# Moving VectorE's part of the weights' decoding within a unit of work, in a top-k attention and cosine feed-forward kernel on one Trainium2 core

## The chip, the cores and the metric

The kernel runs on one core of one Trainium2 chip. A core has five engines that run side by side, each through its own list of instructions in order: TensorE (PE, with its weight loads shown apart as PEld), VectorE (DVE), ScalarE (ACT), GpSimd (POOL) and SyncE (SP), which here only issues transfers. They wait for each other through semaphores. The metric is the device time of one execution in microseconds (us); lower is better. The figure for the kernel before is the median of several runs, 1549.34 us. The profile is of one further execution.

## The reference

There are two stages. For every one of 8 x 8 pairs of batch and head, attention over 576 positions keeps the 32 highest scores of each row. Its output, laid out as 4608 rows (tokens) of 512, goes through a feed-forward layer with 2048 hidden columns whose gate is `h * cos(h)`.

```python
scores = (1 / sqrt(D)) * matmul(q, k.transpose(0, 1, 3, 2))      # D = 64, S = 576
kth = partition(scores, -32)[..., -32]
scores = where(scores >= kth, scores, -1e9)
scores = scores - max(scores)
attn = exp(scores)
attn = attn / (sum(attn) + 1e-9)
x = matmul(attn, v)              # brought to (4608, 512)
h = x @ w_in                     # (512, 2048)
out = (h * cos(h)) @ w_out       # (2048, 512)
```

`q`, `k` and `v` arrive as float32. The two weight matrices arrive as 64-bit floats; the kernel turns them into float32 itself. This is "the decoding".

## The kernel before

**Units and slots.** A unit is 128 rows (tokens) of two heads: 36 blocks of 128 tokens by 4 pairs of heads give 144 units. The loop runs once for each unit and once more; a turn of it is called a slot. What the engines do in a slot, and in which order, is written out by hand: the order of the calls in `early_slot`, `slot` and `last_slot` is the order of each engine's instructions. Slots 0 to 12 are `early_slot` (`EARLY = 3 * NP = 12`), slots 13 to 140 `slot`, the last four `last_slot`. In slot i the unit u = i has its top-k search made; w is unit i - 1, which had its search in the slot before and is now finished.

**The search (VectorE).** `topk_first(u, w)` folds the 576 scores of each row in two halves of 288 (L244, one maximum and one minimum, read from PSUM and from ScalarE's copy in SBUF), closes the threshold of the unit before (`merge_first` L292, `merge_second` L297), and makes the first round of the search: `MAX8` (L304) gives the eight largest, `MATCH_REPLACE8` (L307) strikes them out. `topk_round(u, 1)`, `(u, 2)` and `(u, 3)` are the other rounds.

**Finishing the unit before.** `bounds`, `mask` and `exponentials` are ScalarE's (L314, L317, L326, L334); they end with `den` at L339. VectorE's `reciprocal` (L343) turns `den` into `rden`. GpSimd's `normalise` (L348) waits for it; then in early slots TensorE transposes the result (`transposes_now`, L382), ScalarE copies it out of PSUM (L386, L389), TensorE multiplies it with the values (L408), and ScalarE copies that out (`take_values`, L414). In ScalarE's list that copy stands ahead of `bounds` of the next slot. So from one reciprocal to the next there runs a loop through GpSimd, TensorE and ScalarE.

**The decoding.** There are 32 chunks of 128 x 512 (16 of `w_in`, 16 of `w_out`), and each goes through four stations. `load_weights(n)` issues up to n transfers on SP's queue into staging tiles (L116). `decode_first(n)` is three ScalarE activations for a chunk (L126 to L128). `decode_second(n)` is two VectorE `tensor_scalar` instructions for a chunk: a maximum with 2.0 (L137), in place on the float32 chunk, and a shift left by 3 (L138), in place on the same bits. `decode_third()` is two GpSimd `tensor_tensor` for every chunk that has had its second part (L147, L148). It stands in GpSimd's list behind `normalise` and `gate`. Of the chunks, slot 0 decodes three, slots 1 to 5 three each, slots 6 to 12 two each: 3 + 15 + 14 = 32. After slot 12 nothing is left to decode.

**GpSimd's list in an early slot** is therefore: `normalise` (L348, twice), `gate` (L530) where there is one, `decode_third`, then `reduce_first` (L504, L505, L506) and `reduce_second` (L513) where a tile of hidden columns is ready. After that it waits for the next slot's reciprocal.

**The feed-forward part** is spread over the slots by `feed`, which takes as many steps as a credit allows. All these choices are made while the program is built, so the order of the instructions does not depend on how long anything takes.

Of the kernel before, what the change touches and what calls it, by code (L numbers as in the profile page):

```python
# [31 lines left out]
def kernel(  # L32
# [70 lines left out]
    def load_weights(n):  # L103
        for _ in range(n):
            i = wq["next"]
            if i >= len(chunks):
                return
            src, dst = chunks[i]
            if not DECODE:
                nc.sync.dma_start(out=dst, in_=src)  # L110
                wq["next"] = wq["done"] = i + 1
                continue
            if staged() + ff["live"] >= CHUNKS:
                return
            st = ffw.tile([P, CW, 2], I32, tag="g", name="st", bufs=CHUNKS)
            nc.sync.dma_start(out=st.rearrange("p w i -> p (w i)"), in_=src)  # L116
            wq["loaded"].append((st, dst))
            wq["next"] = i + 1
# [12 lines left out]
    def decode_second(n):  # L131


        for _ in range(min(n, len(wq["second"]))):
            st, w = wq["second"].popleft()
            wi = w.bitcast(I32)
            nc.vector.tensor_scalar(out=w, in0=w, scalar1=2.0, scalar2=None, op0=ALU.max)  # L137
            nc.vector.tensor_scalar(  # L138
                out=wi, in0=wi, scalar1=3, scalar2=None, op0=ALU.logical_shift_left
            )  # L140
            wq["third"].append((st, w))

    def decode_third():
        while wq["third"]:
            st, w = wq["third"].popleft()
            wi = w.bitcast(I32)
            nc.gpsimd.tensor_tensor(out=wi, in0=wi, in1=st[:, :, 0], op=ALU.add)  # L147
            nc.gpsimd.tensor_tensor(out=w, in0=w, in1=st[:, :, 1].bitcast(F32), op=ALU.mult)  # L148
            wq["done"] += 1
# [63 lines left out]
    def scores(u):  # L213
        sc = u["sc"] = ps.tile([P, 2, 512], F32, tag="sc", name="sc", bufs=2)
        for to, k0, k1 in ((sc, 0, SB), (sc_ends[u["n"] % 2], SB, S)):
            for j in range(2):
                d = slice(j * D, (j + 1) * D)
                for b, q0, rows, r0 in u["parts"]:
                    st = pairs[b, u["hp"]]
                    nc.tensor.matmul(  # L220
                        to[r0 : r0 + rows, j, 0 : k1 - k0],
                        st["q"][d, q0 : q0 + rows],
                        st["k"][d, k0:k1],
                        start=True,
                        stop=True,
                    )

    def take_scores(u):
        s = u["s"] = work.tile([P, 2, S], F32, tag="s", name="s", bufs=4)
        nc.scalar.copy(out=s[:, :, 0:SB], in_=u["sc"][:, :, 0:SB])  # L230
        nc.scalar.copy(out=s[:, :, SB:S], in_=sc_ends[u["n"] % 2])  # L231
        if not u["folds"]:
            del u["sc"]
# [23 lines left out]
    def topk_first(u, w):  # L257

        u["top"] = tops[u["n"] % len(tops)]
        merges = [merge_first, merge_second] if w and w["folds"] else []  # L260
        if u["folds"]:
            for op in (ALU.max, ALU.min):
                fold(u, op)
                if merges:
                    merges.pop(0)(w)
        else:
            u["rest"] = work.tile([P, 2, S], F32, tag="rest", name="rest", bufs=1)
        for merge in merges:
            merge(w)
        topk_round(u, 0)  # L270

    def topk_round(u, rnd):
        top, rest, lasts = u["top"], u["rest"], TOPK // 8 - 1
        end = TOPK - 1 - 8 * rnd
        at = top[:, :, end : end - 8 if rnd < lasts else None : -1, 0]
        if u["folds"]:
            search(at, rest[:, :, 0:HS], rest[:, :, 0:HS], rnd < lasts)
            if rnd < TOPK // 16:

                low = top[:, :, 1 + 8 * rnd : 9 + 8 * rnd, 1]  # L280
                search(low, rest[:, :, HS:S], rest[:, :, HS:S], rnd < TOPK // 16 - 1)
        else:
            search(at, u["s"] if rnd == 0 else rest, rest, rnd < lasts)
        if rnd == lasts:
            del u["rest"]
# [23 lines left out]
    def bounds(u):  # L309

        ends = u.pop("top").rearrange("p j r i -> p j (r i)")
        ends = ends[:, :, 2 * TOPK - 2 :] if u["folds"] else ends[:, :, 2 * TOPK - 2 :: 2 - 2 * TOPK]
        nb = u["nb"] = small.tile([P, 2, 2], F32, tag="nb", name="nb")
        nc.scalar.mul(out=nb, in_=ends, mul=-SCALE)  # L314
        nd = u["nd"] = small.tile([P, 2], F32, tag="nd", name="nd")
        for j in range(2):
            nc.scalar.activation(  # L317
                out=nd[:, j : j + 1], in_=ends[:, j, 1:2], func=AF.Identity,
                bias=nb[:, j, 0:1], scale=SCALE,
            )  # L320

    def mask(u):

        s, nb = u["s"], u.pop("nb")
        for j in range(2):
            nc.scalar.activation(  # L326
                out=s[:, j], in_=s[:, j], func=AF.Prelu, bias=nb[:, j, 1:2], scale=SCALE, alpha=FAR
            )

    def exponentials(u):  # L330
        s, nd = u["s"], u.pop("nd")
        den = u["den"] = small.tile([P, 2], F32, tag="den", name="den")
        for j in range(2):
            nc.scalar.activation(  # L334
                out=s[:, j], in_=s[:, j], func=AF.Exp, bias=nd[:, j : j + 1], scale=1.0,
                accum_out=den[:, j : j + 1],
            )

        nc.scalar.activation(out=den, in_=den, func=AF.Identity, bias=eps, scale=1.0)  # L339

    def reciprocal(u):
        u["rden"] = small.tile([P, 2], F32, tag="rden", name="rden")
        nc.vector.reciprocal(u["rden"], u.pop("den"))  # L343

    def normalise(u):
        s, rden = u["s"], u.pop("rden")
        for j in range(2):
            nc.gpsimd.tensor_scalar(  # L348
                out=s[:, j], in0=s[:, j], scalar1=rden[:, j : j + 1], scalar2=1.0,
                op0=ALU.mult, op1=ALU.mult,  # L350
            )
# [130 lines left out]
    def take_banks():  # L482
        while full:
            take, *what = full.popleft()
            take(*what)
# [22 lines left out]
    def reduce_second():  # L508
        if not fresh or len(fresh[0]) < 3:
            return  # L510
        blk, g, x = fresh.popleft()
        if not ff["end"]:
            nc.gpsimd.tensor_tensor(out=x, in0=g, in1=x, op=ALU.subtract)  # L513
        waiting.append((blk, g, x, ff["now"], -TWO_PI_BELOW if ff["end"] else TWO_PI_BELOW))
# [11 lines left out]
    def gate(n):  # L526
        for _ in range(min(n, len(sined))):
            blk, g, x = sined.popleft()
            eng = nc.vector if ff["end"] else nc.gpsimd
            eng.tensor_tensor(out=g, in0=g, in1=x, op=ALU.mult)  # L530
            blk["gated"].append(ff["tick"])
# [81 lines left out]
    for n in range(NP, len(order)):  # L613
        i = last[order[n - 5]] if n >= 5 else 0
        at_slot.setdefault(max(i, NP + 2), []).append((load_qk, *order[n]))
        i = last_values[order[n - 6]] if n >= 6 else 0
# [12 lines left out]
    def early_slot(i, u, w):  # L629
        n = 3 if i < 6 else 2  # L630
        topk_first(u, w)
        decode_second(1 if i == 0 else n)
        scores(units[i + 1])
        for load, b, hp in at_slot.get(i, []):
            load(b, hp)
        load_weights(n)
        if w:
            bounds(w)
            mask(w)
            exponentials(w)  # L640
        topk_round(u, 1)
        if i == 0:
            decode_second(2)
        if w:
            reciprocal(w)
        topk_round(u, 2)
        topk_round(u, 3)
        if w:
            normalise(w)
        take_banks()  # L650
        take_scores(units[i + 1])
        gate(1)
        decode_third()
        feed(2)
        reduce_first()
        reduce_second()
        if i != NP:
            decode_first(n - 1)
        if w:
            transposes_now(w)  # L660
        feed(1)
        decode_first(n - len(wq["second"]))
        if w:
            values([w])
            take_values([w])
        feed(2)
        sines(1)
# [167 lines left out]
```

## Time and profile before

| | |
|---|---|
| time, median of 7 runs | 1549.34 us (1546.88 to 1551.63) |
| time of the profiled execution | 1556.08 us |
| its span, first to last instruction | 1554.3 us |
| TensorE's mean granted clock in it | 0.947 of full speed |
| ACT busy | 1171.3 us, 75% of the span |
| POOL busy | 1097.1 us, 71% of the span |
| L137, 32 instructions | 411 ns at least, 1368 ns at most |
| L138, 32 instructions | 426 ns at least, 2458 ns at most |

The profiled execution lies 6.7 us above the median of the runs, and 1.8 us of it lie outside its span. An engine's busy time counts an instruction from its start to its end, so time in which an instruction stands blocked inside the engine counts as busy. A timeline gives for each instruction its start and its duration in us, then engine, line and operation, then what it writes and reads; what stands in brackets is the engine's idle time ahead of it and what ended that. Spans on POOL are rough.

In the profiled execution the early slots begin (first fold of VectorE) at 7.63, 20.72, 32.67, 46.41, 60.17, 73.92, 88.20, 102.15, 117.57, 132.98, 150.83, 163.58 and 179.00 us; slot 13 begins at 193.47 us.

### The profile page before, as it was taken

The page shows a single profiled execution, that of the slowest core. Times are in us where ns is not written, and L with a number is a line of the kernel's source. Part 1 is how long each engine was busy: PE and PEld are TensorE (multiplying, and loading weights), DVE is VectorE, ACT ScalarE, POOL GpSimd, SP SyncE. Part 2 cuts the span into 40 slices and gives each one's busy share as a digit, 9 for nine tenths or more (in the row PEclk, how much of TensorE's full clock was granted, in tenths as well). Part 3 has the DMA queues.
Part 4 walks back from the last instruction along what each step waited for, and adds up shares of the span by engine and source line. Part 5 has one row for each costly group of instructions (what it writes and reads, how often), then busy time and mean ns, then how long its engine had stood idle before and what let it go on. Part 6 is the DMA issues. An engine that isn't in the chain of part 4 may idle for free.

```text
span 1554.3 us, 30369 instructions
## 1 busy us (share of the span) xinstructions
PE 1438.4 (93%) x10396; PEld 1031.2 (66%) x10396; DVE 1428.1 (92%) x4809; ACT 1171.3 (75%) x2342; POOL 1097.1 (71%) x834
## 2 busy tenths in 40 slices
PE   4477798999999999999999999999999999999999
PEld 3364565667667776777677776777677776777675
DVE  7998986999999998999999998999999999999831
ACT  7788775788778886788788886888788887888651
POOL 4666675777777777777777776777777777777510
PEclk6587988999999999999999999999999999999999
DMA  8331136545654456545655455545654455544300
GB/s 255 111 109 41 42 72 171 137 137 150 184 161 130 130 146 169 147 132 153 181 143 134 139 148 160 153 137 145 180 147 137 129 147 173 145 130 130 83 8 14
DMA packets 361835, 207.51 MB, mean 134 GB/s; under 512 B 311888, under 2 KB 328528, under 8 KB 361680
## 3 DMA queue, kind: packets, MB, share of 16 engines
q1 hardware_dynamic: 356272, 195.91, 45.5%
q10 hardware_dynamic: 5408, 9.65, 1.7%
q8 instruction: 82, 1.34, 0.4%
q14 instruction: 73, 0.60, 0.1%
HBM read 45.09 MB, written 84.93 MB: 84 GB/s over the span
## 4 chain that ended last, share of the span: by engine, by line
POOL 31%; DVE 26%; PE 21%; issue 10%; ACT 6%; DMA 5%; SPq 1%; POOLq 0%; ACTq 0%; DVEq 0%
DVE top L304 10%; POOL halves L360 8%; DVE rest L307 8%; PE mm L465 7%; PE o L543 7%; POOL s L348 6%; POOL g L530 5%; POOL x L513 4%; DVE rest L244 4%; PE rim L408 3%; PE sc L220 3%; DMA pT<-rows 2%; POOL x L506 2%; POOL x L505 2%; DMA rows<-halves 2%
## 5 line engine op out<-in xcount | busy, mean ns | idle before, releaser
L304 DVE MAX8 top<-rest 128x8 f32<-128x288 f32 x1716 | 692.7, 457 | 0.0
L465 PEld LDWEIGHTS mm<-xT,w_in 128*128 128x128 f32 x4608 | 542.8, 194 | 69.8 <-issue 62.4
L543 PE MATMUL o<-w_out,g 128*128 128x512 f32 x1152 | 546.3, 608 | 7.4 <-POOL g L530 3.9
L465 PE MATMUL mm<-xT,w_in 128*128 128x128 f32 x4608 | 546.4, 277 | 2.6 <-ACT g L478 2.5
L307 DVE MATCH_REPLACE8 rest<-top,rest 128x288 f32<-128x288 f32 x1144 | 504.3, 452 | 0.0
L348 POOL TENSOR_SCALAR s<-s,rden 128x576 f32<-128x576 f32 x288 | 212.4, 749 | 330.5 <-DVE rden L343 323.0
L543 PEld LDWEIGHTS o<-w_out,g 128*128 128x128 f32 x1152 | 204.8, 192 | 199.9 <-issue 183.4
L360 POOL COPY halves<-s 128x2304 uint16<-128x2304 uint16 x128 | 269.3, 2104 | 9.5 <-DMA rows<-halves 1.5
L244 DVE TENSOR_TENSOR rest<-sc,s 128x576 f32<-128x576 f32 x284 | 213.8, 753 | 39.1 <-ACT s L231 31.1
L334 ACT ACTIVATE s<-s,nd 128x576 f32<-128x576 f32 x288 | 220.5, 767 | 1.2 <-ACT ob L553 0.4
L326 ACT ACTIVATE s<-s,nb 128x576 f32<-128x576 f32 x288 | 206.0, 763 | 0.0
L408 PE MATMUL rim<-pT,v 128*64 128x128 f32 (+1 forms) x2560 | 166.8, 276 | 29.2 <-DMA pT<-rows 19.4
L408 PEld LDWEIGHTS rim<-pT,v 128*64 128x64 f32 x2560 | 137.0, 143 | 84.5 <-issue 39.6
L220 PE MATMUL sc<-k,q 64*128 64x448 f32 (+1 forms) x640 | 160.1, 605 | 13.2 <-DVE w_in L138 7.1
L530 POOL TENSOR_TENSOR g<-g,x 128x1024 f32<-128x1024 f32 x68 | 160.8, 2364 | 7.4 <-ACT nb L314 4.0
L513 POOL TENSOR_TENSOR x<-g,x 128x1024 f32<-128x1024 f32 x68 | 160.8, 2364 | 5.7
L478 ACT ACTIVATE g<-mm 128x512 f32<-128x512 f32 x144 | 84.6, 588 | 93.9 <-PE mm L465 88.0
L230 ACT COPY s<-sc 128x896 f32<-128x896 f32 x144 | 129.6, 900 | 4.9 <-PE sc L220 4.9
L414 ACT COPY xT<-rim 128x256 f32<-128x256 f32 (+1 forms) x80 | 28.0, 350 | 111.6 <-PE rim L220 92.7
L523 ACT ACTIVATE x<-x,halfpi 128x1024 f32<-128x1024 f32 x72 | 83.0, 1152 | 25.2 <-POOL x L513 17.9
L220 PEld LDWEIGHTS rim<-k,q 64*128 64x128 f32 (+1 forms) x640 | 59.7, 187 | 61.3 <-issue 56.4
L307 DVE MATCH_VALUE_LOAD rest<-top,rest 128x8 f32 x1144 | 96.6, 84 | 0.0
(55 smaller groups left out, 1261.5 us busy)
## 6 DMA issues: line engine op xcount, KB each, us to landing
rows<-halves SPq DMA_DIRECT2D x128, 576.0 KB, 2.8
out_dram<-ob ACTq DMA_DIRECT2D x36, 256.0 KB, 2.7
q<-in_q_dram SPq DMA_DIRECT2D x31, 288.0 KB, 3.4
st<-in_moe_w_in_dram SPq DMA_DIRECT2D x16, 512.0 KB, 5.2
v<-in_v_dram SPq DMA_DIRECT2D x32, 256.0 KB, 3.2
st<-in_moe_w_out_dram SPq DMA_DIRECT2D x16, 512.0 KB, 3.6
k<-in_k_dram SPq DMA_DIRECT2D x31, 144.0 KB, 3.5
k<-in_k_dram SPq DMA_DIRECT2D x32, 128.0 KB, 3.4
```

What stands on the lines that cost most here:

```text
L220: nc.tensor.matmul(to[r0 : r0 + rows, j, 0 : k1 - k0], st["q"][d, q0 : q0 + rows], st["k"][d, k0:k1], start=True, stop=True,)
L244: nc.vector.tensor_tensor(out=u["rest"][:, :, i * HS : (i + 1) * HS], in0=sc[:, :, 0:HS], in1=s[:, :, HS:S], op=op,)
L304: nc.vector.max(to[:, j], src[:, j])
L307: nc.vector.match_replace(rest[:, j], to[:, j], src[:, j], NEG)
L334: nc.scalar.activation(out=s[:, j], in_=s[:, j], func=AF.Exp, bias=nd[:, j : j + 1], scale=1.0, accum_out=den[:, j : j + 1],)
L348: nc.gpsimd.tensor_scalar(out=s[:, j], in0=s[:, j], scalar1=rden[:, j : j + 1], scalar2=1.0, op0=ALU.mult, op1=ALU.mult,)
L360: nc.gpsimd.tensor_copy(out=halves, in_=s.rearrange("p (k h) -> p h k", h=2))
L408: nc.tensor.matmul(o[d, to], lhsT, rhs, start=c == 0, stop=c == NT)
L465: nc.tensor.matmul(mm[:, at : at + w], w_in[f // FC][:, c, (f % FC) * P : (f % FC + 1) * P], blk["xT"][:, c], start=c == 0, stop=c == NC - 1,)
L513: nc.gpsimd.tensor_tensor(out=x, in0=g, in1=x, op=ALU.subtract)
L530: eng.tensor_tensor(out=g, in0=g, in1=x, op=ALU.mult)
L543: nc.tensor.matmul(o, g[:, at : at + P], w_out[f], start=f == 0, stop=f == NF - 1)
```

## The change

`decode_second` is called from another place in `early_slot`. In slots 1 to 12 it stood directly behind `topk_first`; it now stands behind `topk_round(u, 1)`, directly ahead of `reciprocal(w)`. In slot 0 one chunk is still decoded behind `topk_first` and the other two behind round 1, as before. The arguments give the same number of chunks in each slot. Nothing else differs: no instruction is added or removed, and on ScalarE, GpSimd, TensorE and SP the order is the same.

```diff
     def early_slot(i, u, w):
         n = 3 if i < 6 else 2
         topk_first(u, w)
-        decode_second(1 if i == 0 else n)
+        if i == 0:
+            decode_second(1)
         scores(units[i + 1])
         for load, b, hp in at_slot.get(i, []):
             load(b, hp)
...
             mask(w)
             exponentials(w)
         topk_round(u, 1)
-        if i == 0:
-            decode_second(2)
+
+        decode_second(n)
         if w:
             reciprocal(w)
         topk_round(u, 2)
```

## The prediction

> **What bounds the kernel now.** I read the page's engines and its 40 slices of 38.9 us first:
>
> ```profile
> PE 1438.4 (93%) x10396; PEld 1031.2 (66%) x10396; DVE 1428.1 (92%) x4809; ACT 1171.3 (75%) x2342; POOL 1097.1 (71%) x834
> PE   4477798999999999999999999999999999999999
> DVE  7998986999999998999999998999999999999831
> ```
>
> From slice 8 on PE and DVE are both dense. In the early slots, up to 193 us, PE is half idle and DVE nearly full. So the change is priced in those slots, and what they save moves the dense rest as a whole. Next I took the windows of DVE from the first decode instruction of a slot to the first one after (start:end, length, DVE busy, granted PE clock, DMA); here those of slots 4, 7 and 12:
>
> ```profile
> 64.87:69.07 4.20, 4.10 (x7) 0.50 0.59 165
> 106.86:112.73 5.87, 5.80 (x6) 0.95 0.30 89
> 183.71:185.31 1.60, 1.53 (x6) 0.97 0.00 0
> ```
>
> Slot 12 decodes two chunks in 1.60 us, and slot 1 three in 2.39: 0.80 us a chunk. Slot 7 takes 5.87 us for two, with DVE shown busy. The timelines of DVE and POOL in slot 7 say what it does there:
>
> ```profile
> 106.86 1.10 DVE L137 TENSOR_SCALAR w_out<-w_out 128x512 f32<-128x512 f32 x1
> 108.00 1.14 DVE L138 TENSOR_SCALAR w_out<-w_out 128x512 int32<-128x512 int32 x1
> 109.06 1.25 DVE L137 TENSOR_SCALAR w_out<-w_out 128x512 f32<-128x512 f32 x1
> 110.35 2.46 DVE L138 TENSOR_SCALAR w_out<-w_out 128x512 int32<-128x512 int32 x1
> 115.03 0.15 DVE L343 RECIPROCAL rden<-den 128x2 f32<-128x2 f32 x1
> ```
>
> ```profile
> 106.64 1.05 POOL L504 TENSOR_SCALAR x<-g 128x1024 f32<-128x1024 f32 x1
> 107.77 1.09 POOL L505 TENSOR_SCALAR x<-x 128x1024 f32<-128x1024 f32 x1
> 108.94 1.10 POOL L506 TENSOR_SCALAR x<-x 128x1024 f32<-128x1024 f32 x1
> 110.12 2.40 POOL L513 TENSOR_TENSOR x<-g,x 128x1024 f32<-128x1024 f32 x1
> 115.35 1.48 POOL L348 TENSOR_SCALAR s<-s,rden 128x576 f32<-128x576 f32 x2 [2.83 <-DVE rden L343]
> ```
>
> Each decode instruction ends about 0.3 us after the POOL instruction that was running when it started; alone it takes 0.42. It is blocked by POOL. Then POOL idles 2.83 us until the reciprocal. Last, the waits at the reciprocal: in slots 5, 6, 9 and 12 DVE is early and ScalarE's `den` comes last (0.43, 0.78, 5.01, 3.21 us); here slots 5, 9 and 12:
>
> ```profile
> 85.64 0.17 DVE L343 RECIPROCAL rden<-den 128x2 f32<-128x2 f32 x1 [0.43 <-ACT den L339]
> 148.26 0.17 DVE L343 RECIPROCAL rden<-den 128x2 f32<-128x2 f32 x1 [5.01 <-ACT den L339]
> 190.91 0.17 DVE L343 RECIPROCAL rden<-den 128x2 f32<-128x2 f32 x1 [3.21 <-ACT den L339]
> ```
>
> **What the Trainium skill says.** "SBUF — State Buffer", section Who interferes with whom: DVE shares a pair of SBUF ports with GpSimd; a `tensor_scalar` in a two-port mode takes it for the whole instruction, and whichever issued first blocks the other fully. The trace agrees (2.46 us for 0.42 us of work). "VectorE: DVE Perf Modes", What auto-detection actually checks: a one-source op between SBUF tensors gets two-port mode; L137 and L138 are such, and L307, with nearly equal times beside a working POOL, shows no blocking (0.45 us in both conditions). "Perfetto Trace Analysis", GPSIMD Engine Instruction: POOL spans are to be timed by start-to-start spacing; I do so, 1.25 us from L148 to the next L147 although L148's record says 1.30. "TensorE: Matmul & The Clock Gate", What's actually happening: PE halves its clock after some 3.4 us of idleness; here clock 0.50 in slots 1 to 5 agrees.
>
> **The change part by part.** Slot 0 keeps its order, and no instruction is added; SP's queue, ScalarE's and POOL's lists stay. Loads, `decode_first` and `decode_third` hang on the same things: `decode_third` stands behind `normalise`, which waits for the reciprocal, and the reciprocal stays behind the decoding. Moving round 1 ahead costs nothing: nobody waits for its result before the next slot, and it is not blocked by POOL. Round 1 lasts 2.30 us (69.07 to 71.37). So the decoding starts 2.30 us later relative to the POOL work that the previous reciprocal released, and the reciprocal follows it at once.
>
> The blocked time per slot is the window less 0.80 us a chunk: 1.80 in each of slots 2 to 5 (4.2 less 2.4), 1.92 in slot 6, 4.28 in each of 7, 8 and 11 (5.87 less 1.59), 1.6 in each of 9 and 10, none in 1 and 12: 25.2 us. How much can be had is decided by two things: does POOL still work 2.30 us later, and is `den` there.
>
> Slots 2 to 4. In slot 4 the decoding would start at 64.87 + 2.30 = 67.17; POOL's last L148 starts at 65.93 and, by spacing, frees the ports at 67.18. A tie, the same in 2 and 3 (39.67 and 39.67, 53.42 and 53.43), and a lost tie costs up to 0.3. ScalarE is no limit: from reciprocal to `den` it needs 11.1 us (57.62 to 68.74), DVE then 13.75 - 1.80 = 11.95. Gain 3 x 1.8 = 5.4.
>
> Slot 5. From reciprocal 71.37 through POOL, transposes, ScalarE copies, three chunks of `decode_first` (75.76 to 81.47, all behind the copies in slot 4), L414 and the exponentials to `den` it is 14.17 us, all hung on that reciprocal. The stall at POOL goes, and a longer wait for `den` takes its place. Gain 0. Slot 6 likewise: the loop takes 13.95 us, with TensorE's feed-forward matmuls ahead of the transposes. Gain 0.
>
> Slot 7. The decoding starts at 109.16, in L506. The first L137 ends with it, at 110.2; the first L138 meets L513 and ends at about 112.7, as the last one does now; the second chunk then runs free, 0.80. The reciprocal comes at 113.48 instead of 115.03. Gain 1.55.
>
> Slot 8. DVE would gain 1.55 again, but ScalarE has a sine with two table loads here: `den` is ready 15.04 us after the reciprocal before, plus 0.1 to the next. 15.41 less 15.14 leaves 0.27. Slot 9: `den` needs 17.8 us (5.01 idle now). Gain 0.
>
> Slot 10. The decoding starts at 157.83; POOL's L148, started at 156.38, is over by 157.7. `den` was there at 158.52; the reciprocal comes at 159.43 instead of 161.03. Gain 1.6. Slot 11 has slot 7's pattern: 1.55 more; `den`, at 172.13, is not late.
>
> Slot 12 is bound by the loop. TensorE's transposes waited for POOL until 177.59; 3.15 us earlier they meet TensorE's own matmuls, which end at 175.25 and hang on an earlier reciprocal. So they come only 2.34 earlier: -0.8. But TensorE then isn't idle for 2.3 us, and may do the next 20 matmuls at full clock (1.31 us as in slot 11, 166.19 to 167.50, instead of 2.40): +1.1, of which ScalarE's list lets some 0.65 through. Between -0.8 and -0.15 I take -0.5.
>
> Sum: 5.4 + 1.55 + 0.27 + 1.6 + 1.55 - 0.5 = 9.9 us at the reciprocal of slot 12. From there everything hangs on that reciprocal (PE stood idle 5.65 us for it, POOL 7.7), so the rest of the span moves with it. 1554.3 becomes 1544.4, the profiled execution 1546.2. That execution lies 6.7 us above the median; a saving of early time shows in both alike: 1549.34 - 9.9 = 1539.4.
>
> The unknowns. Lost ties: -0.9. Slot 12: from -0.3 to +0.35. TensorE warm a little sooner elsewhere: 0 to +2. So 8.7 to 12.3, a range of its own of 1537 to 1540.7, and 1.5 either way for the spread of medians: 1535.5 to 1542.2.
>
> **The rivals.** *All blocked time pays*: 25.2 us, 1524.1. For it: DVE is shown busy in these slots. Against: the four waits for `den`. *The dense part swallows it*: if something not hung on slot 12's reciprocal, a transfer or TensorE's backlog, sets the pace after 206 us, the gain ends near 0, 1549; swallowed by half, 1544. For it: the chain of waits shows DMA pieces of 4 to 7 us near 590, 640 and 760 us. Against: those come after hundreds of us of fixed-order work, and their transfers are issued by the shifted queues. *Slower, by TensorE's clock*: the windows from 300 to 1480 us show granted clocks of 0.98 to 1.00. If the new timing puts idle gaps at places where the clock then falls, each 0.01 of mean clock over these 1180 us costs 11.8 us; from 0.0084 on it outweighs the gain, at 0.015 the time is 1549.3 - 9.9 + 17.7 = 1557. For it: early slots show clock 0.50 after gaps. Against: the change shortens gaps. *The change doesn't clear the ports*, since the tie falls to POOL and each instruction meets the next one of it: at most what is paid now, so no loss, 1547 to 1549.
>
> **How the numbers follow.** Forecast 0.68. All blocked time, or well above 13 us: 0.06. Half swallowed (3 to 7 us): 0.11. Swallowed, or ports not cleared: 0.08. Slower by the clock: 0.07. 0.2% is 3.1 us, about what a measurement of this kernel can tell from no change. Faster: 0.68 + 0.06 + 0.11 = 0.85; same 0.08; slower 0.07. For 8 in 10 the range takes in the forecast's own range and the better part of the half-swallowed case: 1534.5 to 1545.
>
> **What would show it.** Right: windows of the decoding of 2.4 us in slots 2 to 5 and 1.6 in 6 and 10; in 7, 8 and 11 still a blocked L137 and L138; waits for `den` of some 2 us in slots 5 and 6; slot 13's fold at about 183.6 instead of 193.47; POOL's idle time ahead of L348 shorter. Wrong in a step: decoding still blocked in slots 2 to 4; `den` late where I have DVE last; a fold of slot 13 moved by 10 us with an end that isn't.

## The result and the profile after

The changed kernel takes 1539.02 us (median of 12 runs, 1534.14 to 1546.04) against 1548.93 us for the kernel before beside it (31 runs, 1543.95 to 1553.43). The ratio is 0.9936, 95% interval 0.9922 to 0.9951: 9.9 us less, with 7.6 to 12.1 as the interval. The forecast was 1539.4. A second measurement of the same two kernels gave 1541.42 against 1548.32 us, 6.9 us less (4.8 to 12.4; row 11 in the table of experiments). So that it is faster is sure; the agreement with the forecast to a tenth is not a finding.

First the decoding of each slot after the change: windows of VectorE from its first decode instruction to the reciprocal, or to the end of the decoding where VectorE then waits (start:end, length, DVE busy, PE clock, DMA). These are slots 2, 4, 5, 6, 8, 10 and 11.

```profile
39.20:41.58 2.38, 2.28 (x7) 0.99 0.72 210
63.52:65.92 2.40, 2.30 (x7) 1.00 0.52 178
76.15:78.55 2.40, 2.30 (x7) 0.50 1.21 229
90.42:92.04 1.62, 1.55 (x5) 1.00 0.48 154
118.08:122.35 4.27, 4.20 (x5) 0.86 0.09 36
150.53:152.12 1.59, 1.52 (x5) 1.00 0.52 113
161.68:165.97 4.29, 4.22 (x6) 1.00 0.00 0
```

Three chunks take 2.4 us and two take 1.6 wherever GpSimd has nothing left to do. Slots 8 and 11 (and 7) still lose 2.7 us. The timelines of VectorE and GpSimd in slot 7 show why:

```profile
104.26 1.07 DVE L137 TENSOR_SCALAR w_out<-w_out 128x512 f32<-128x512 f32 x1
105.36 2.45 DVE L138 TENSOR_SCALAR w_out<-w_out 128x512 int32<-128x512 int32 x1
107.73 0.41 DVE L137 TENSOR_SCALAR w_out<-w_out 128x512 f32<-128x512 f32 x1
108.18 0.43 DVE L138 TENSOR_SCALAR w_out<-w_out 128x512 int32<-128x512 int32 x1
108.53 0.16 DVE L343 RECIPROCAL rden<-den 128x2 f32<-128x2 f32 x1
```

```profile
104.00 1.05 POOL L506 TENSOR_SCALAR x<-x 128x1024 f32<-128x1024 f32 x1
105.13 2.40 POOL L513 TENSOR_TENSOR x<-g,x 128x1024 f32<-128x1024 f32 x1
108.86 1.48 POOL L348 TENSOR_SCALAR s<-s,rden 128x576 f32<-128x576 f32 x2 [1.33 <-DVE rden L343]
```

Two of GpSimd's four feed-forward instructions (L504, L505) are over before the decoding starts; the other two (L506, L513) each block one decode instruction; the second chunk runs free. GpSimd's idle time ahead of L348 is 1.33 us instead of 2.83.

What VectorE no longer spends blocked it partly spends waiting. These are the reciprocals of slots 3 to 6 in VectorE's timeline after:

```profile
53.95 0.17 DVE L343 RECIPROCAL rden<-den 128x2 f32<-128x2 f32 x1 [0.34 <-ACT den L339]
66.58 0.17 DVE L343 RECIPROCAL rden<-den 128x2 f32<-128x2 f32 x1 [0.59 <-ACT den L339]
80.85 0.17 DVE L343 RECIPROCAL rden<-den 128x2 f32<-128x2 f32 x1 [2.22 <-ACT den L339]
94.69 0.17 DVE L343 RECIPROCAL rden<-den 128x2 f32<-128x2 f32 x1 [2.57 <-ACT den L339]
```

Slots 5 and 6 waited 0.43 and 0.78 us before, slots 3 and 4 not at all. All the starts of L343, put side by side, give the interval from the reciprocal of the slot before to that of the slot itself, in us:

| slot | 2 | 3 | 4 | 5 | 6 | 7 | 8 | 9 | 10 | 11 | 12 | sum |
|---|---|---|---|---|---|---|---|---|---|---|---|---|
| before | 13.74 | 13.76 | 13.75 | 14.27 | 13.95 | 15.44 | 15.41 | 17.82 | 12.77 | 15.44 | 14.44 | 160.79 |
| after | 11.95 | 12.37 | 12.63 | 14.27 | 13.84 | 13.84 | 15.16 | 17.27 | 11.16 | 13.85 | 14.24 | 150.58 |
| saved | 1.79 | 1.39 | 1.12 | 0 | 0.11 | 1.60 | 0.25 | 0.55 | 1.61 | 1.59 | 0.20 | 10.21 |
| forecast | 1.8 | 1.8 | 1.8 | 0 | 0 | 1.55 | 0.27 | 0 | 1.6 | 1.55 | -0.5 | 9.87 |

The sum of a row, from the reciprocal of slot 1 to that of slot 12, is the yardstick of the experiments. The rows before and after are one execution each. In a second profiled execution of the changed kernel, slot 3 took 12.05 instead of 12.37 and slot 9 17.42 instead of 17.27; the other slots agree within 0.1 us, and the sum is 150.19. Slot 13's first fold came at 182.77 us instead of 193.47; 183.6 was forecast.

The two profiled executions themselves differ by more, 1554.3 against 1536.3 us of span. At the reciprocal of slot 12 (190.91 and 180.21) the difference is 10.7, at that of slot 14 12.6, at the last one (1493.62 and 1475.60) 18.0. Where it goes beyond 10.7 the two lists of instructions are the same. In the second profiled execution of the changed kernel the last reciprocal lies at 1482.11, 6.5 us later than in the first. So single profiles of one kernel drift apart by some microseconds in the dense part, and only the medians tell what reaches the end.

### The profile page after: what moved, and what is told of

Its sections match the earlier page's. It is cut to its first block, busy times and chain, and to the rows that moved or that the text cites. A ratio compares the mean times of both kernels' runs of the same rounds, so it can differ in the third digit from the quotient of the medians.

```text
span 1536.3 us, 30369 instructions
## 1 busy us (share of the span) xinstructions
PE 1425.6 (93%) x10396; PEld 1024.3 (67%) x10396; DVE 1411.2 (92%) x4809; ACT 1171.1 (76%) x2342; POOL 1096.4 (71%) x834
## 4 chain that ended last, share of the span: by engine, by line
POOL 43%; PE 14%; issue 13%; ACT 11%; DVE 10%; DMA 7%; SPq 2%; POOLq 0%; ACTq 0%; DVEq 0%
POOL halves L360 12%; POOL s L348 9%; POOL g L530 7%; POOL x L513 6%; DVE top L304 4%; PE mm L465 4%; PE o L543 4%; DVE rest L307 4%; POOL x L505 3%; POOL x L506 3%; POOL x L504 3%; DMA rows<-halves 3%; DMA pT<-rows 3%; PE rim L408 2%; PE sc L220 2%
## 5 line engine op out<-in xcount | busy, mean ns | idle before, releaser
L348 POOL TENSOR_SCALAR s<-s,rden 128x576 f32<-128x576 f32 x288 | 212.4, 749 | 319.7 <-DVE rden L343 309.7
L408 PE MATMUL rim<-pT,v 128*64 128x128 f32 (+1 forms) x2560 | 165.4, 275 | 34.1 <-DMA pT<-rows 19.8
L408 PEld LDWEIGHTS rim<-pT,v 128*64 128x64 f32 x2560 | 136.0, 142 | 88.6 <-issue 37.2
L220 PE MATMUL sc<-k,q 64*128 64x448 f32 (+1 forms) x640 | 158.8, 605 | 14.1 <-DMA k<-in_k_dram 14.0
L513 POOL TENSOR_TENSOR x<-g,x 128x1024 f32<-128x1024 f32 x68 | 160.8, 2365 | 5.7
L414 ACT COPY xT<-rim 128x256 f32<-128x256 f32 (+1 forms) x80 | 28.0, 350 | 114.6 <-PE rim L220 97.1
L220 PEld LDWEIGHTS rim<-k,q 64*128 64x128 f32 (+1 forms) x640 | 59.3, 187 | 61.2 <-issue 56.1
```

Source lines behind the costliest of these rows:

```text
L220: nc.tensor.matmul(to[r0 : r0 + rows, j, 0 : k1 - k0], st["q"][d, q0 : q0 + rows], st["k"][d, k0:k1], start=True, stop=True,)
L348: nc.gpsimd.tensor_scalar(out=s[:, j], in0=s[:, j], scalar1=rden[:, j : j + 1], scalar2=1.0, op0=ALU.mult, op1=ALU.mult,)
L408: nc.tensor.matmul(o[d, to], lhsT, rhs, start=c == 0, stop=c == NT)
```

## The experiments

The experiments ran in three groups (rows 1, 2, 5 and 6; rows 3, 4, 7 and 8; rows 9 to 12), each on one chip with the kernel before beside it, whose median was 1548.33, 1546.63 and 1548.32 us. "Slot 14" is the start of slot 14's reciprocal, 216.72 us before and 204.15 (205.06 in the second execution) after the change; it is of use where an edit moves the reciprocal itself against the decoding.

| what | yardstick | slot 14 | median | ratio to before |
|---|---|---|---|---|
| moved in slots 1 to 5 only | 156.83 | 209.81 | 1542.50 | 0.9962 (0.9946 to 0.9977) |
| moved in slots 6 to 12 only | 155.85 | 209.96 | 1541.96 | 0.9953 (0.9927 to 0.9978) |
| without `decode_third`, old place | 148.33 | 201.20 | 1532.50 | 0.9919 (0.9894 to 0.9944) |
| without `decode_third`, new place | 147.78 | 200.30 | 1528.15 | 0.9897 (0.9873 to 0.9921) |
| slot 4's `decode_first` split, new place | 149.54 | 204.06 | 1534.97 | 0.9911 (0.9896 to 0.9926) |
| slot 4's `decode_first` split, old place | 160.05 | 215.44 | 1546.61 | 0.9992 (0.9981 to 1.0003) |
| behind the reciprocal | 159.81 | 212.39 | 1541.54 | 0.9968 (0.9957 to 0.9978) |
| behind round 2 | 165.13 | 219.63 | 1546.48 | 1.0000 (0.9986 to 1.0014) |
| behind round 2, last chunk first | 155.43 | 210.43 | 1542.89 | 0.9957 (0.9941 to 0.9973) |
| the same, slot 4's `decode_first` split | 153.88 | 209.64 | 1542.43 | 0.9949 (0.9928 to 0.9969) |
| the change, again | 150.19 | 205.06 | 1541.42 | 0.9944 (0.9920 to 0.9969) |
| the change with slot 4 split, again | 147.87 | 201.57 | 1535.72 | 0.9916 (0.9889 to 0.9943) |

**Which slots pay.** The change was cut in two halves.

```diff
         if i == 0:
             decode_second(1)
+        if i > 5:                 # the other run: if 0 < i < 6
+            decode_second(n)
         scores(units[i + 1])
```

> The decoding is moved in slots 1 to 5 only; in slots 6 to 12 it stays behind topk_first. Yardstick: time from the reciprocal of slot 1 to that of slot 12, 160.79 us before and 150.58 after. Theory (only slots where VectorE comes last pay, slots 2 to 4 by 1.8, 1.4 and 1.1 us): reciprocals of slots 2 to 5 as after, slots 6 to 12 as before, yardstick 156.5, time 1544.6. Rival (every blocked microsecond pays the same share, 7.2 of 25.2 blocked us lie here): 157.9 and 1546.1. Rival (the gain comes from the slots with feed-forward work on GpSimd only): yardstick 160.8, no change.

> The decoding is moved in slots 6 to 12 only; in slots 1 to 5 it stays behind topk_first. Theory: slots 2 to 5 as before, then the savings of slots 7 (1.5), 8 (0.3), 9 (0.5), 10 (1.6), 11 (1.6) and 12 (0.2): yardstick 160.8 - 5.9 = 154.9, time 1543.0; together with the run that moves slots 1 to 5 the two gains add up to that of the whole change. Rival (shares of blocked time, 18 of 25.2 us): 153.5 and 1541.9. Rival (the two halves aren't independent, because the early saving is eaten by a later wait): the sum of the two gains is clearly over or under 9.9.

The yardstick fell by 3.96 and 4.94 us. The first is near the theory (156.5 expected, 156.83 measured). The slots show it better than the sum: slots 2 to 4 gave 1.79, 1.71 and 1.17 us and slot 5 nothing, 4.68 together, although 1.80 us of blocked time went in each of the four. That is not an equal share for all blocked time, nor nothing. But slots 6 to 12, whose order is that of the kernel before, did not stay as before: slot 7 was 0.80 us shorter and slots 8, 9 and 12 were 0.49, 0.41 and 0.67 longer, 0.72 us lost in all. That the sum came so near is partly cancellation. The second is 0.95 short of the theory (154.9): slots 7, 8, 10, 11 and 12 came out within 0.1 us of those of the whole change (13.84, 15.14, 11.16, 13.85, 14.20), but slot 9 took 18.40, 1.13 more than in the first execution of the whole change. The two gains add to 8.90, 10.21 less these 1.13 us to within 0.2. The sums thus speak for halves that are nearly independent; slot by slot the first run shows that moving early slots also shifts the later ones by up to 0.8 us, and why was not followed up. The medians fell by 5.8 and 6.4 us, with intervals of some 5 and 8 us, too wide to tell this.

**Is it GpSimd, or the order of the rounds?** `decode_third` was emptied, in the kernel before and in the changed one.

```diff
             wi = w.bitcast(I32)
-            nc.gpsimd.tensor_tensor(out=wi, in0=wi, in1=st[:, :, 0], op=ALU.add)
-            nc.gpsimd.tensor_tensor(out=w, in0=w, in1=st[:, :, 1].bitcast(F32), op=ALU.mult)
             wq["done"] += 1
```

> The kernel before without GpSimd's two instructions a chunk (L147, L148): the low part and the sign of the weights are left out. Theory (L137 and L138 are blocked by whatever GpSimd is running): with GpSimd idle the decoding takes 2.4 us in slots 2 to 5 and 1.6 in slots 6, 9 and 10 at its old place too; in slots 7, 8 and 11 the feed-forward work starts some 5 us earlier and is nearly over, so one instruction at most is blocked. Yardstick 147 to 150, time 1536 to 1539. Rival (the order of the search rounds is what matters): windows stay at 4.2 us or the yardstick stays near 160.

> The changed kernel without the same GpSimd instructions. Theory: no difference of more than 1 us from the run that leaves them out of the kernel before, since with GpSimd out of the way the place of the decoding does not matter: yardstick 147 to 149. Rival (order matters by itself): about 10 us below that run.

The yardsticks are 148.33 and 147.78, 0.55 apart, where the same move is worth 10.2 us with `decode_third` in place. The decoding at its old place, in VectorE's timeline of the run without `decode_third`, slot 4:

```profile
60.22 0.42 DVE L137 TENSOR_SCALAR w_in<-w_in 128x512 f32<-128x512 f32 x1
60.67 0.43 DVE L138 TENSOR_SCALAR w_in<-w_in 128x512 int32<-128x512 int32 x1
61.01 0.42 DVE L137 TENSOR_SCALAR w_in<-w_in 128x512 f32<-128x512 f32 x1
61.47 0.43 DVE L138 TENSOR_SCALAR w_in<-w_in 128x512 int32<-128x512 int32 x1
```

No decode instruction of the slot is longer than 0.43 us. In all early slots of this run only three are longer than 0.46 us: one each in slots 7, 8 and 11 (0.53 to 0.56), beside GpSimd's last feed-forward instruction. In most slots of both runs VectorE waits for `den`, which could hide an effect of the order. In slots 7 and 10 it does not wait, and there the two runs took 11.28 and 11.17, and 11.18 and 11.16 us. So the place matters only through what GpSimd does meanwhile; having round 1 ahead is worth nothing by itself. The two medians, 1532.5 and 1528.2 with four runs each, have ratios whose intervals overlap. They lie 14.1 and 18.5 us below the kernel before, where the yardsticks explain 12.5 and 13.0, and below the 1536 to 1539 us that were expected; where the rest comes from was not followed up.

**Why slot 5 pays nothing.** In slot 4 alone all three chunks of `decode_first` stand behind the transposes' copies. The edit puts two of them ahead, as in other slots.

```diff
-        if i != NP:
-            decode_first(n - 1)
+        decode_first(n - 1)
         if w:
             transposes_now(w)
```

> The changed kernel, and in slot 4 two of the three chunks of decode_first stand ahead of the transposes' copies, as in other slots. Theory (in slot 5 VectorE waits 2.22 us for den because ScalarE's three chunks lie in the loop from reciprocal to reciprocal): the interval from reciprocal 4 to 5 falls from 14.27 to 12.4 to 12.6, time about 1.8 below the changed kernel, 1537.2. Rival (something else holds that loop, such as the transfers of the weights): the interval stays above 14, ScalarE stands idle ahead of L126, no change or slower.

> The kernel before with the same edit of slot 4. Theory: VectorE, blocked by GpSimd, is the limit at once, so the interval from reciprocal 4 to 5 falls only from 14.27 to about 13.75 (that of slots 2 to 4), time 1548.4, within what can be told from no change. The edit is worth some 1.3 us more on top of the change than without it. Rival (loop not bound there by ScalarE): no difference between the two.

With the change slot 5 fell from 14.27 to 12.64, without it only to 13.74, as expected to within 0.04 us. ScalarE's timeline of slot 4 in the changed kernel with the edit shows what follows the copies now, one chunk instead of three:

```profile
71.12 1.05 ACT L386 COPY pT<-tp 128x512 f32<-128x512 f32 x2
72.06 0.27 ACT L389 COPY pT<-rim 128x128 f32<-128x128 f32 x1
72.22 0.70 ACT L126 ACTIVATE w_out<-st 128x512 f32<-128x512 f32 x1
73.01 0.68 ACT L127 ACTIVATE st<-st 128x512 f32<-128x512 int32 x1
73.59 0.66 ACT L128 ACTIVATE st<-st 128x512 int32<-128x512 uint32 x1
74.86 0.27 ACT L414 COPY xT<-rim 128x128 f32<-128x128 f32 x1 [0.60 <-PE rim L408]
```

The copies start without a wait (2.25 us without the edit), and L414 follows 3.7 us after them instead of 6.8. So the loop through ScalarE held slot 5, and there one edit is worth more on top of the other: 1.63 us instead of 0.53. In the yardstick this is 1.0 against 0.7, because slot 9 of the run with both took 18.40 us.

**Would a later place be better?** First directly behind the reciprocal, then behind round 2.

```diff
-        decode_second(n)
         if w:
             reciprocal(w)
+        decode_second(n)          # the other run: behind topk_round(u, 2), for i > 0
         topk_round(u, 2)
```

> The decoding one instruction later, directly behind the reciprocal. Theory: the reciprocal no longer waits for the blocked decoding in slots 7 and 11, but VectorE's port instructions and GpSimd's normalise now start together and take turns; each normalise may be held up by up to 0.4 us twice, each slot. Where ScalarE's list is the limit (slots 3, 4, 5, 6) nothing is won. Yardstick 147 to 151, time 1536 to 1539.5. Rival (blocking of normalise lengthens the loop through GpSimd in every slot by 0.8 us): yardstick 155 to 159, time 1544 to 1548.

> The decoding behind round 2, when normalise has ended and GpSimd, whose next work is decode_third, can only wait for it. Theory: no blocking in slots 2 to 8, 11 and 12 (windows 2.4 and 1.6 us), up to 2.4 us in slots 9 and 10 where gate runs then; the reciprocals of slots 7, 10 and 11 come up to 2.7, 0.9 and 1.0 us earlier. Yardstick 146 to 148, time 1535 to 1537. Rival (decode_third now starts 1.6 to 2.4 us later and pushes GpSimd's feed-forward work into the next normalise): yardstick 150 or more, no gain over the changed kernel.

Both expectations were wrong, and with them the ranges: yardsticks 159.81 and 165.13, medians 1541.54 and 1546.48. Here the reciprocal has moved ahead of the decoding, so slot 14 tells more than the yardstick: with the decoding behind the reciprocal it came 4.3 us earlier than in the kernel before, with the decoding behind round 2 it came 2.9 us later. Slots 2 to 6 took 14.8 and 15.0 us each, more than in the kernel before. The timelines of VectorE and GpSimd behind round 2, slot 3:

```profile
60.03 0.43 DVE L138 TENSOR_SCALAR w_in<-w_in 128x512 int32<-128x512 int32 x1
60.38 0.42 DVE L137 TENSOR_SCALAR w_in<-w_in 128x512 f32<-128x512 f32 x1
60.83 1.40 DVE L138 TENSOR_SCALAR w_in<-w_in 128x512 int32<-128x512 int32 x1
62.15 1.51 DVE L137 TENSOR_SCALAR w_in<-w_in 128x512 f32<-128x512 f32 x1
63.70 1.40 DVE L138 TENSOR_SCALAR w_in<-w_in 128x512 int32<-128x512 int32 x1
```

```profile
60.55 1.40 POOL L147 TENSOR_TENSOR w_in<-w_in,st 128x512 int32<-128x512 int32 x1 [0.88 <-DVE w_in L138]
62.03 1.35 POOL L148 TENSOR_TENSOR w_in<-w_in,st 128x512 f32<-128x512 f32 x1
63.34 1.47 POOL L147 TENSOR_TENSOR w_in<-w_in,st 128x512 int32<-128x512 int32 x1
```

GpSimd waits only for the first chunk's L138. As soon as it has that, its own work on that chunk blocks VectorE's work on the second and third. The decoding, blocked by its own consumer, takes 5.4 us instead of 2.4. Behind the reciprocal the same happens at the third chunk (1.52 and 1.39 us in slot 3); the second is held up a little by `normalise` (0.85 and 0.77), and `normalise` itself takes 1.97 us instead of 1.47. Ahead of the reciprocal it can't: `decode_third` stands behind `normalise`, which waits for the reciprocal, and so for all chunks.

If that is the reason, it should be enough to let GpSimd begin with the chunk that is decoded last.

```diff
         while wq["third"]:
-            st, w = wq["third"].popleft()
+            st, w = wq["third"].pop()
```

> The decoding behind round 2, and GpSimd takes the chunks of a slot in reverse, the last decoded first. Theory (behind round 2 the first finished chunk let GpSimd start, which then blocked the other chunks' VectorE instructions): GpSimd now can't start before the last chunk is through, so the windows are 2.4 and 1.6 us again, the intervals of slots 2 to 4 fall from 15.0 to 12.0 to 12.6, yardstick 148 to 153, time 1537 to 1541. Rival (the place behind round 2 is bad for another reason, such as a later GpSimd or a late fold): intervals stay near 15, yardstick near 165, time 1546.

> The run before with the edit of slot 4 (two chunks of decode_first ahead of the transposes' copies). Theory: slot 5 falls from about 14.2 to 12.6 as it did in the changed kernel; yardstick 147 to 151.5, time 1535 to 1539.5. Rival: GpSimd, which now ends its work later in a slot, holds slot 5 up, no gain from the edit.

Slots 2 to 4 fell to 12.46, 12.58 and 12.61, with no blocked decode instruction, and slots 7 and 11 even to 11.19 and 11.17. So the reason was right. Yet the yardstick, 155.43, stayed above the 148 to 153 expected, and the median, 1542.89, above 1537 to 1541: slots 8 and 12 took 18.48 and 17.73. GpSimd's timeline in slot 7, where the reciprocal started at 104.18:

```profile
103.94 1.04 POOL L506 TENSOR_SCALAR x<-x 128x1024 f32<-128x1024 f32 x1
105.06 2.37 POOL L513 TENSOR_TENSOR x<-g,x 128x1024 f32<-128x1024 f32 x1
107.41 2.05 POOL L348 TENSOR_SCALAR s<-s,rden 128x576 f32<-128x576 f32 x2
```

`normalise` begins 3.2 us after its reciprocal, because GpSimd's work of the slot before, begun later, isn't done. The rival named for the place behind round 2 is thus true of the slots with feed-forward work. The edit of slot 4 brought slot 5 from 14.23 to 12.64 here too, but yardstick and median (153.88 and 1542.43) missed their ranges as well.

**The best version.** The changed kernel and the one with the edit of slot 4 ran once more on one chip.

> The changed kernel once more, beside the runs of this call on one chip: 9.9 us less than the kernel before, 1538 to 1540, yardstick 150.6 to 152 (slot 9 may be 17.3 or 18.4 long, by when TensorE's clock rises).

> The changed kernel with the edit of slot 4, beside the changed kernel on one chip: 1 to 2.5 us less than it by the sum (1.6 in slot 5, up to 0.4 in slot 3, up to 1.1 lost in slot 9); if the 4 us between their earlier medians were the edit's, 3 us or more.

The medians are 1541.42 and 1535.72 us. The changed kernel gained 6.9 us where 9.9 were expected, and its yardstick, 150.19, lies just under the 150.6 to 152 expected. The edit of slot 4 is ahead by 4.1 us in the earlier measurements (1539.02 and 1534.97, not taken on one chip) and by 5.7 us here, and of the versions that leave nothing out it has the lowest ratio both times, 0.9911 and 0.9916. The intervals of the ratios overlap in both pairs. The yardsticks give it 1.0 and 2.3 us, of which 1.6 in slot 5; 1 to 2.5 us were expected from the sum. That it is faster is likely, by how much stays open.

## Why the prediction was right

**The mechanism.** Blocking by GpSimd: right, shown by the runs without `decode_third`. That the ports are the reason is what the page "SBUF — State Buffer" of the Trainium skill says, section Who interferes with whom: of a VectorE instruction in a two-port mode and a GpSimd instruction, the one that comes second fully blocks. The runs agree without showing the ports: in the early slots of all 14 profiles each L137 or L138 over 0.46 us runs beside a GpSimd instruction.

**Slots 2 to 4.** The tie with GpSimd's last L148 was won each time (windows of 2.38 to 2.40 us). The size was too high in two of them: 1.39 and 1.12 instead of 1.8 (1.71 and 1.18 in the second execution). The term at fault is ScalarE's 11.1 us from reciprocal to `den`. That was a latency measured while ScalarE was idle ahead of the transposes' copies. In the shorter slots 2 and 3 ScalarE has no idle time there, and its own list of instructions, with three chunks of `decode_first` and 0.6 us of waiting for TensorE ahead of L414, takes 12.6 us from `den` to `den` (L339 at 41.01, 53.62 and 66.25). Slot 2, at 11.95, was still VectorE's; in slots 3 and 4 `den` was 0.34 and 0.59 us late. That cost 1.1 us. In the second execution `den` ran with the same period (40.35, 52.93 and 65.50) but came earlier against VectorE, so that slot 3 did not wait for it, slot 4 waited 0.52 us, and the cost was 0.7.

**Slots 5 and 6.** Right: 0 and 0.11, and the waits for `den` are 2.2 and 2.6 us where some 2 were forecast. That ScalarE's three chunks hold slot 5 is shown by the pair of runs with slot 4 edited. For slot 6 the cause was only read from the timelines.

**Slots 7, 8, 10 and 11.** Right to 0.05 us: 1.60, 0.25, 1.61 and 1.59 for 1.55, 0.27, 1.6 and 1.55. The pattern of the blocked instructions in slot 7 was the one forecast.

**Slots 9 and 12.** Forecast 0 and -0.5, measured 0.55 and 0.20. In slot 12 TensorE stayed at full clock, as held possible: its values' matmuls took 1.09 us instead of 1.97. But 0.20 lies above even the best case that was named, -0.15. The transposes began 0.82 us later after their reciprocal, as forecast, and the stretch from the values' matmuls to those of the next scores (L408 to L220) was 1.08 us shorter. So nearly all of the 1.1 us came through to the reciprocal, not the 0.65 assumed. Slot 9 is not shown to be a gain of the change, see the last section. Together these two made good the 1.1 us lost in slots 3 and 4, so that the sum came out right partly by luck.

**What reaches the end.** By the medians 9.9 us in the first measurement and 6.9 in the second, of 10.2 and 10.6 us in the yardsticks. That 9.9 was met to a tenth is luck: the intervals are some 5 and 8 us wide. The rival that the dense part swallows the whole gain falls; that it swallows half falls by the first measurement (at least 7.6 us), while the second (at least 4.8) leaves room for it. "All blocked time" (1524.1) falls, and so does "slower by TensorE's clock": the granted clock from 300 to 1480 us was 0.98 to 1.00 before and 0.99 after. The mean clock of the two profiled executions, 0.947 and 0.959, tells nothing by itself, since single executions of the kernel before lie between 0.947 and 0.972.

## What to carry to other kernels

A VectorE instruction that GpSimd blocks, as L137 and L138 here, is better put where GpSimd's list is waiting than where VectorE's own data are ready first; look for the GpSimd instruction that waits for VectorE and stand directly ahead of its releaser. Make sure that GpSimd can't start on the first piece while VectorE is still at the others, since such a consumer blocks its own producer (5.4 us instead of 2.4 behind round 2). And when a slot gets shorter, check each other engine's whole list for the slot, not only its latency from the last wait.

## What the runs showed of the hardware

Slot 9 varied from 16.97 to 18.40 us between two executions of one and the same kernel. These two are the executions of the changed kernel with slot 4's `decode_first` split. In both, TensorE has stood idle for 7.2 to 7.3 us before it transposes (L382), and 0.9 us after the transposes it starts four matmuls. The first three lines are from TensorE's timeline of the slower, the other three from that of the faster:

```profile
122.96 1.12 PE L382 MATMUL tp<-ident,s 128*128 128x128 f32 x4 [7.32 <-POOL s L348]
126.03 3.78 PE L543 MATMUL o<-w_out,g 128*128 128x512 f32 x4 [0.89 <-POOL g L530]
129.74 1.98 PE L408 MATMUL rim<-pT,v 128*64 128x128 f32 x16
```

```profile
122.60 1.12 PE L382 MATMUL tp<-ident,s 128*128 128x128 f32 x4 [7.24 <-POOL s L348]
125.66 3.44 PE L543 MATMUL o<-w_out,g 128*128 128x512 f32 x4 [0.88 <-POOL g L530]
129.03 1.09 PE L408 MATMUL rim<-pT,v 128*64 128x128 f32 x16
```

The 16 matmuls behind them took 1.98 us in one and 1.09 in the other. The granted clock was 0.50 in both when the four started; in the slower execution it rose only after 132.0 us, 6 us later and behind the 16, in the faster at about 128.6, 3 us later and ahead of them. A loop that hangs on TensorE at such a point carries an uncertainty of over a microsecond that no edit of these runs controls; a prediction can only widen its range by it.

The other finding is how blocking runs when both engines have several instructions ready: they take turns, one by one. In the kernel before, slot 7's four decode instructions each lasted to about 0.3 us past the GpSimd instruction that ran when they began. The loss is therefore up to one GpSimd instruction for each VectorE instruction, 4.3 us on 1.6. GpSimd loses far less there: L505 and L506 took 1.09 and 1.10 us between the decode instructions, and 1.05 without them.
